# Weight conversion without a maximum and a mask, with a new set of planner settings

## The chip, the cores and the metric

The kernel runs on one NeuronCore of one Trainium2 chip. The core has TensorE for matrix products (PE in the rows, and PEld for its loading of weights), VectorE (DVE), ScalarE (ACT), GpSimd (POOL), and SyncE (SP), whose queue issues every DMA here. The metric is the time of one execution on the device in microseconds (us). Three timed runs of the kernel before took 1967.29, 1968.99 and 1971.42 us, the median being 1968.99 us.

## The reference, cut to what matters

Three layers follow each other. x is 2304 tokens by 512.

```python
x = attention(q, k, v)            # local window of 7 keys, plus attention on means of 4 tokens
h = np.maximum(x @ w_in, 0.0)     # first layer, 512 -> 2048
x = h * h @ w_out                 # 2048 -> 512
P = exp(x @ w_gate - max)         # gates of 8 experts, 8 rounds of balancing rows and columns
for e in range(8):                # second layer
    out += P[:, e:e+1] * (np.maximum(x @ w1[e], 0.0) @ w2[e])
```

The inputs `w_in` and `w_out` of the first layer reach the kernel as 64-bit words (in the host's layout they are viewed as int64, since they are float64), so that the kernel turns each pair of 32-bit words into a float32 itself. This is the weight conversion that the change is about.

## The kernel before, in words

Every fp32 product is made of three products of a high and a low part: the high part is ScalarE's rounding copy, the low part is the rest, a subtraction on VectorE or GpSimd. Tokens are worked in five blocks (`BLOCKS`, j = 0 to 4, of 512, 512, 512, 384 and 384 tokens), and the hidden width of the first layer in 16 pieces of 128 (fc = 0 to 15).

For each block there is an attention part. Blocks 0 and 1 take the local attention on TensorE (`local_pe`, lines 672 to 780, which ends with the matmuls of line 776), blocks 2 to 4 on VectorE (`local_v`, lines 802 to 896, which ends with the transposes of line 867). Attention on the means of four tokens (`down_pair`, lines 555 to 616) has per pair of heads the scores (line 564), three exponentials on ScalarE (line 575), two transposes (line 594) with a ScalarE copy each (line 596), and the product with v (line 609), which ScalarE copies to `od` (line 614). Then come the two products of the first layer (`l1_first`, line 1026; `l2_first`, line 1069), which ScalarE and VectorE join (lines 1041 to 1045). The second layer (`l1_second`, line 1462, and `l2_second`, line 1748) starts when block 4 is done; it needs weights that `units_weights` loads, adds up (line 1284) and splits (line 476), 32 units in all, and for each unit 3 passes of 42 matmuls, with VectorE and ScalarE taking each pass out of PSUM (lines 1529 to 1559).

The conversion of one piece fc (`convert`) loads the 64-bit words of both matrices into one of two buffers `o` (line 936), takes the absolute value of the upper words (ScalarE, line 944), and puts the float32 together on VectorE in four steps (lines 946, 948, 950, 952). Then ScalarE makes the high part `f` (line 957) and VectorE or GpSimd the low part `s` (line 960), which is also stored to DRAM (line 965) and loaded again for the later blocks (line 982).

The order of the instructions on every engine is made when the program is built. `Order` keeps a list of processes, gives each operation the earliest start that a table of costs allows, and writes the instructions down in that order. An engine carries out its list in order, so an instruction that waits holds all that stand behind it on its engine; this includes SP's list of DMAs. The settings of this planner that the diff touches are `AHEAD` (how many pieces ahead the stored low parts are loaded again), `X1FIRST` (how many of four inputs of a block must be there before its first product starts), `NEARLY` (pieces from this number on are converted only after block 0's attention in the plan), `LATE` (by how many ns GpSimd may end later than VectorE and still be given an operation; used in `convert` and `units_weights`) and `SLACK_PE` (ns that TensorE's work of blocks 1 to 4's attention and of the balancing of gates is put later in the plan). Costs that differ also move what is written down.

Of the kernel before, what the change touches and what calls it, by code (L numbers as in the profile page):

```python
# [11 lines left out]
F32 = mybir.dt.float32  # L12
# [4 lines left out]
AF = mybir.ActivationFunctionType  # L17
ALU = mybir.AluOpType
# [23 lines left out]
SCALE = 1.0 / 8.0  # L42
NEG = -1e9

LEAST = float(np.array([896 << 20], np.int32).view(np.float32)[0])

# [26 lines left out]

NVA, NVD, NQD, NDE, NPT = 1, 2, 2, 2, 2

AHEAD, WARM, X1FIRST = 3, 4, 3

NEARLY = 3  # L80

PUT_OFF, PACE = (1, 2, 4), 1


LATE, SLACK, SLACK_PE = 500.0, 100.0, 0.0
LATE_A = 0.0

BOOT_NS, BOOT_DMA = 40000.0, 1.7
# [278 lines left out]
def _dma(nbytes):  # L367
    return ("op", "DMA", nbytes / 360.0)
# [10 lines left out]
def _w2p(n, late=0.0):  # L379
    return ("op", ("V2", "PL"), (148.0 + n * 1.05, 170.0 + n * 2.26), late)  # L380
# [7 lines left out]
def tile_kernel(ctx: ExitStack, tc, qh, kp, vp, qn, kn, vn, vd, bias, mask, w_in, w_out, wg, w12, out):  # L388
    nc = tc.nc
    V, A, PE, PL = nc.vector, nc.scalar, nc.tensor, nc.gpsimd  # L390
# [53 lines left out]
    def get(sl, dt=F32, shape=None, least=1):  # L444
        return ("get", sl, dt, shape, least)
# [478 lines left out]
    def early_half(fc):  # L924
        return int(fc < NF // 2)

    def at_item(j, fc):
        return lambda: (progress["j"], progress["fc"]) >= divmod(j * NF + fc, NF)

    def convert(fc):  # L930

        yield ("need", at_item(0, fc - 5) if fc >= 5 else lambda: len(shared) >= min(NHP, fc + 1))
        raw = yield get(s_boot, I64, [128, 2, 512])
        for i, w in enumerate((w_in, w_out)):
            yield _dma(128 * 4096)
            dma(out=raw[:, i], in_=w[fc])
        if fc >= NEARLY:
            yield ("wait", ev_x1[0][NHP - 1])
        words = raw.bitcast(I32).rearrange("p i (f two) -> p i f two", two=2)
        low, high = words[:, :, :, 0], words[:, :, :, 1]  # L940
        x = yield get(s_x1, F32, None, lambda: 1 + NHP - xs_taken[0])
        xi = x.bitcast(I32)
        yield ("op", "A", 1146)
        A.activation(out=x, in_=raw.bitcast(F32).rearrange("p i (f two) -> p i f two", two=2)[:, :, :, 1], func=AF.Abs)
        yield ("op", "V2", 680)
        V.tensor_scalar(out=x, in0=x, scalar1=LEAST, scalar2=None, op0=ALU.max)
        yield ("op", "V2", 680)
        V.tensor_scalar(out=xi, in0=xi, scalar1=3, scalar2=0x3FFFFFFF, op0=ALU.logical_shift_left, op1=ALU.bitwise_and)
        yield ("op", "V2", 1220)
        V.scalar_tensor_tensor(out=xi, in0=high, scalar=-0x40000000, in1=xi, op0=ALU.bitwise_and, op1=ALU.bitwise_or)  # L950
        yield ("op", "V2", 1220)
        V.scalar_tensor_tensor(out=xi, in0=low, scalar=29, in1=xi, op0=ALU.logical_shift_right, op1=ALU.bitwise_or)
        s_boot.put(raw)
        order.fire(ev_f[fc])
        hi = yield get(s_wf[early_half(fc)], F32R)
        yield ("op", "A", 1146)
        A.activation(out=hi, in_=x, func=AF.Copy)
        lo_ = yield get(gen, F32R)
        eng = ENG[(yield _w2p(1024, LATE))]
        eng.tensor_tensor(out=lo_, in0=x, in1=hi.bitcast(F32), op=ALU.subtract)  # L960
        s_x1.put(x)
        his[fc], los[0, fc] = hi, lo_
        order.fire(ev_w[0, fc])
        yield _dma(128 * 4096)
        dma(out=scr_w[fc], in_=lo_.bitcast(F32))
        order.fire(ev_scr[fc])
        drop_w(0, fc)
# [21 lines left out]
    def drop_w(j, fc):  # L989
        uses[j, fc] -= 1  # L990
        if uses[j, fc] == 0:
            gen.put(los.pop((j, fc)))
# [886 lines left out]
    for fc in range(NF):  # L1879
        order.add(convert(fc), 5.0 + 0.1 * fc)  # L1880
# [63 lines left out]
```

## Time and profile before

| what | value |
|---|---|
| timed runs | 1967.29, 1968.99, 1971.42 us, median 1968.99 us |
| the profiled execution's own time | 1970.68 us |
| its span, from the first to the last instruction | 1968.6 us |
| mean granted TensorE clock | 0.990 of full speed |
| TensorE busy | 1938.3 us (98%) |
| VectorE busy | 1413.1 us (72%) |
| ScalarE busy | 825.0 us (42%) |
| GpSimd busy | 169.8 us (9%) |
| DMA moved | 476.56 MB, mean 242 GB/s |

The profiled execution's own time is 2.1 us over its span and 1.7 us over the median of the timed runs. Busy shares are means over stages with different limits. TensorE's 98% holds filler matmuls too (line 1827, until the first layer starts) and stretches in which the clock was at half speed. A difference of 0.2%, some 3.9 us, is about what a measurement of this kernel tells from none.

### The profile page before, as it was taken

Reading aid. Unit: us, or ns where it says so; the run is one execution under the profiler, and the core shown is the slowest. Engines: PE = TensorE matmul, PEld = TensorE weight load, DVE = VectorE, ACT = ScalarE, POOL = GpSimd, SP = SyncE. Lnnn points to the kernel's source line nnn. Section 1 sums busy time; section 2 is a strip of 40 time slices with the busy share of each in tenths; the row PEclk is TensorE's granted clock in tenths of the full one; section 3 lists DMA queues with packets and bytes.
Section 4 is the critical chain, followed back from the end, with each engine's and each line's share of the span. In section 5 each row is a group of like instructions: output and inputs, shape, how many; then the busy total and the mean of one; then the engine's idle time right before and its main releaser. Section 6 shows DMA issues by size and latency. Waiting matters only on the chain.

```text
span 1968.6 us, 30220 instructions
## 1 busy us (share of the span) xinstructions
PE 1938.3 (98%) x11213; PEld 1841.5 (94%) x11213; DVE 1413.1 (72%) x2002; ACT 825.0 (42%) x1489; POOL 169.8 (9%) x193
## 2 busy tenths in 40 slices
PE   9899989999989999999999999999999999999999
PEld 5677777899989999999999999999999999999998
DVE  6986888883385777777777777777667877666642
ACT  5775443344443222222222222456544454544441
POOL 2101020000001111111111111000001300000000
PEclk9899998999989999999999999999999999999999
DMA  7777665555425665766676666999989999978771
GB/s 205 263 251 243 206 214 172 171 188 199 161 106 202 233 228 209 254 213 229 216 246 224 217 231 230 329 340 336 313 291 339 362 366 336 329 252 276 236 221 49
DMA packets 255148, 476.56 MB, mean 242 GB/s; under 512 B 22248, under 2 KB 163608, under 8 KB 255000
## 3 DMA queue, kind: packets, MB, share of 16 engines
q1 hardware_dynamic: 255000, 474.63, 71.1%
q8 instruction: 88, 1.44, 0.3%
q14 instruction: 60, 0.49, 0.1%
HBM read 306.44 MB, written 168.11 MB: 241 GB/s over the span
## 4 chain that ended last, share of the span: by engine, by line
PE 92%; DMA 4%; DVE 2%; issue 1%; ACT 1%; SPq 0%; POOL 0%; ACTq 0%; DVEq 0%; POOLq 0%
PE b L1462 35%; PE b L1748 34%; PE b L1026 9%; PE b L1069 8%; PE b L1827 1%; DMA r<-scr_h 1%; DMA lk<-in_kp_dram 1%; DMA scr_r<-t 1%; PE b L564 1%; PE b L609 1%; DMA s<-scr_w 0%; PE b L704 0%; PE b L776 0%; DMA o<-in_w_out_dram 0%; PE b L752 0%
## 5 line engine op out<-in xcount | busy, mean ns | idle before, releaser
L1462 PE MATMUL b<-x,w 128*128 128x384 f32 x2112 | 397.2, 338 | 2.4 <-DVE x L476 1.8
L1462 PEld LDWEIGHTS b<-x,w 128*128 128x128 f32 x2112 | 370.2, 189 | 3.6 <-DVE x L476 2.6
L1069 PE MATMUL b<-g,f 128*128 128x512 f32 (+1 forms) x640 | 200.1, 373 | 0.6 <-ACT t L1095 0.6
L1026 PE MATMUL b<-x,f 128*128 128x512 f32 (+1 forms) x640 | 192.1, 381 | 1.5 <-DVE g L1045 1.5
L1462 PE MATMUL b<-xa,w 128*128 128x384 f32 x960 | 188.0, 335 | 0.0
L1529 ACT ACTIVATE b<-b 128x384 f32<-128x384 f32 x96 | 45.6, 475 | 319.8 <-PE b L1462 319.7
L1462 PEld LDWEIGHTS b<-xa,w 128*128 128x128 f32 x960 | 168.4, 188 | 0.3
L1535 ACT ACTIVATE q<-b 128x384 f32<-128x384 f32 x192 | 94.1, 490 | 164.4 <-PE b L1462 162.8
L1748 PE MATMUL b<-q,w 128*128 128x384 f32 x748 | 161.5, 336 | 0.0
L1559 DVE TENSOR_TENSOR q<-b,q 128x384 f32<-128x384 f32 x96 | 53.5, 558 | 117.9 <-PE b L1462 117.9
L1026 PEld LDWEIGHTS b<-x,f 128*128 128x128 f32 x640 | 117.9, 192 | 18.7 <-DVE g L1045 2.8
L1069 PEld LDWEIGHTS b<-g,f 128*128 128x128 f32 x640 | 118.7, 188 | 17.6 <-ACT t L1095 1.2
L1748 PEld LDWEIGHTS b<-q,w 128*128 128x128 f32 x748 | 132.3, 188 | 0.0
L1748 PE MATMUL b<-xa,w 128*128 128x384 f32 x600 | 127.0, 335 | 0.0
L1284 POOL TENSOR_TENSOR w<-w 128x256 f32<-128x256 f32 x60 | 49.9, 831 | 815.5 <-PE b L1462 608.3
L1041 ACT ACTIVATE b<-b 128x512 f32<-128x512 f32 (+1 forms) x160 | 86.8, 542 | 75.8 <-PE b L1026 71.0
L1462 PE MATMUL b<-xc,w 128*128 128x384 f32 x576 | 115.8, 335 | 0.0
L1548 DVE SCALAR_TENSOR_TENSOR q<-b,gp 128x384 f32<-128x384 f32 x178 | 98.7, 555 | 11.5 <-PE b L1462 8.1
L1748 PEld LDWEIGHTS b<-xa,w 128*128 128x128 f32 x600 | 106.0, 188 | 0.0
L1462 PEld LDWEIGHTS b<-xc,w 128*128 128x128 f32 x576 | 101.4, 188 | 0.0
L476 DVE TENSOR_TENSOR q<-r,q 128x768 fp32r<-128x768 f32 x75 | 71.9, 960 | 35.6 <-ACT q L474 35.3
L474 ACT ACTIVATE q<-r 128x768 fp32r<-128x768 f32 x75 | 63.4, 846 | 76.5 <-PE b L1748 35.9
(292 smaller groups left out, 3867.9 us busy)
## 6 DMA issues: line engine op xcount, KB each, us to landing
r<-scr_h SPq DMA_DIRECT2D x240, 384.0 KB
scr_h<-q SPq DMA_DIRECT2D x89, 576.0 KB
gp<-scr_h SPq DMA_DIRECT2D x96, 384.0 KB
scr_h<-q SPq DMA_DIRECT2D x178, 192.0 KB
scr_h<-q SPq DMA_DIRECT2D x89, 384.0 KB
s<-scr_w SPq DMA_DIRECT2D x43, 512.0 KB
w<-in_w_dram SPq DMA_DIRECT2D x64, 256.0 KB
v<-in_w_dram SPq DMA_DIRECT2D x27, 512.0 KB
```

The lines of the kernel that those rows point to most:

```text
L474: A.activation(out=hi, in_=x, func=AF.Copy)
L476: eng.tensor_tensor(out=lo_, in0=x, in1=hi.bitcast(F32), op=ALU.subtract)
L1026: PE.matmul(ps[:, 0:n], lhsT=w[a][:, c], rhs=x[:, b, 0:n], start=(cc == 0 and i == 0), stop=(cc == 3 and i == 2))
L1041: A.activation(out=s, in_=s, func=func)
L1069: PE.matmul(acc[dc][:, 0:n], lhsT=w[a][:, c], rhs=g[:, b, 0:n], start=(fc == 0 and i == 0), stop=(fc == NF - 1 and i == 2))
L1284: eng.tensor_tensor(out=out, in0=in0, in1=in1, op=op)
L1462: PE.matmul(bank[:, 0:TN], lhsT=w[a][:, iw % 4, cc * 128:cc * 128 + 128], rhs=x[:, b, cc], start=(first and cc == 0 and i == 0), stop=(cc ...
L1529: A.activation(out=ps[1][:, 0:TN], in_=ps[0][:, 0:TN], func=AF.Copy)
L1535: A.activation(out=c[:, place], in_=ps[bank][:, 0:TN], func=AF.Copy)
L1548: V.scalar_tensor_tensor(out=c[:, i], in0=ps[bank][:, 0:TN], scalar=0.0, in1=p[:, 0], op0=ALU.max, op1=ALU.mult)
L1559: V.tensor_tensor(out=c[:, 2], in0=ps[0][:, 0:TN], in1=c[:, 2], op=ALU.add)
L1748: PE.matmul(ps[pb][d][:, 0:TN], lhsT=w[a][:, q, d * 128:d * 128 + 128], rhs=h[:, b, q % 2], start=(first and q == 0 and m == 0), stop=(las ...
```

## The change

ScalarE now multiplies the absolute value of the upper words by 2^-112 (`DOWN`), which moves the exponent from the one bias to the other. The maximum of line 946 goes, the mask `0x3FFFFFFF` in the shift goes, and the sign is now taken with the mask -0x80000000 alone. Per piece, VectorE has three steps in place of four, so 16 instructions on 128x1024 elements fewer. One line less in the file moves every later line number by one: line 1026 becomes 1025, 957 becomes 956, and so on.

Five planner settings change as well.

```diff
-LEAST = float(np.array([896 << 20], np.int32).view(np.float32)[0])
+DOWN = 2.0 ** -112
...
-AHEAD, WARM, X1FIRST = 3, 4, 3
-
-NEARLY = 3
+AHEAD, WARM, X1FIRST = 4, 4, 2
+
+NEARLY = 4
...
-LATE, SLACK, SLACK_PE = 500.0, 100.0, 0.0
+LATE, SLACK, SLACK_PE = 1000.0, 100.0, 600.0
...
-        A.activation(out=x, in_=raw.bitcast(F32).rearrange("p i (f two) -> p i f two", two=2)[:, :, :, 1], func=AF.Abs)
+        A.activation(out=x, in_=raw.bitcast(F32).rearrange("p i (f two) -> p i f two", two=2)[:, :, :, 1], func=AF.Abs,
+                     scale=DOWN)
         yield ("op", "V2", 680)
-        V.tensor_scalar(out=x, in0=x, scalar1=LEAST, scalar2=None, op0=ALU.max)
-        yield ("op", "V2", 680)
-        V.tensor_scalar(out=xi, in0=xi, scalar1=3, scalar2=0x3FFFFFFF, op0=ALU.logical_shift_left, op1=ALU.bitwise_and)
+        V.tensor_scalar(out=xi, in0=xi, scalar1=3, scalar2=None, op0=ALU.logical_shift_left)
         yield ("op", "V2", 1220)
-        V.scalar_tensor_tensor(out=xi, in0=high, scalar=-0x40000000, in1=xi, op0=ALU.bitwise_and, op1=ALU.bitwise_or)
+        V.scalar_tensor_tensor(out=xi, in0=high, scalar=-0x80000000, in1=xi, op0=ALU.bitwise_and, op1=ALU.bitwise_or)
```

All engines' lists differ from the first conversions on. Three places matter for what follows.

**TensorE, at the start of the first layer.** In the names, `b6` is PSUM bank 6, which serves the attention on means at this point; `de0_114` are the weights of a pair of heads of that attention that ScalarE has already made. Before, the scores of the next pair (line 564) were written to bank 6 right behind the first nine products of line 1026 and four filler matmuls:

```order
L564 MATMUL b6_161_906<-dp1_135_790,qd1_81 96x144 x3
L704 MATMUL b7_154_891<-pk0_145_841,pq0_144_840 64x70 x8
L706 LDWEIGHTS ident_b_91
L706 MATMUL b7_154_891<-mask_sb_93,ident_b_91 128x280
L1026 MATMUL b5_143_829<-x6_146_845,f1_0_133_779 128x512 x2
```

The transposes of the pair `de0_114` into the same bank came 33 matmuls of the first layer later, one right after the other:

```order
L1026 MATMUL b5_176_988<-x6_146_845,s2_171_961 128x512
L594 MATMUL b6_184_1026<-ident_84,de0_114_649 72x96 x3
L594 MATMUL b6_187_1040<-ident_84,de0_114_649 72x96 x3
L609 MATMUL b6_191_1052<-pt0_170_956,dv1_99_596 64x144 x4
L564 MATMUL b6_195_1068<-dp0_178_1002,qd0_80 96x144 x3
L1026 MATMUL b4_198_1079<-x0_54_385,f1_3_188_1047 128x512 x2
```

Now the transposes stand at the place of those scores, ahead of them, with six or more products between the steps:

```order
L594 MATMUL b6_158_904<-ident_84,de0_114_649 72x96 x3
L1025 MATMUL b5_140_816<-x6_146_849,f1_0_133_772 128x512 x2
L1025 MATMUL b5_140_816<-x6_146_849,s0_136_793 128x512
L1025 MATMUL b4_162_941<-x0_54_385,f1_1_148_854 128x512 x2
L1025 MATMUL b4_162_941<-x0_54_385,s1_155_886 128x512
L1025 MATMUL b4_162_941<-x2_102_605,f1_1_148_854 128x512 x2
L1025 MATMUL b4_162_941<-x2_102_605,s1_155_886 128x512
L594 MATMUL b6_163_944<-ident_84,de0_114_649 72x96 x3
```

The bank is thus read by the older pair first, and the next pair's scores follow later.

**SP, the loads of piece 3.** In the names, `o` is a buffer of 64-bit words, and `scr_w_111<-s_155` (before: `s_155_897`, now `s_155_886`) is the store of piece 1's low part. Before, the second half of piece 3's load (`o_150`, from `w_out`) stood behind that store and three loads for the attention:

```order
L936 DMA o_150_880<-in_w_in_dram 128x512
L497 DMA dr_156_901<-in_qn_dram 128x576
L497 DMA dr_162_916<-in_kn_dram 128x576
L508 DMA vd_163_922<-in_vd_dram 72x1024
L965 DMA scr_w_111<-s_155_897 128x1024
L936 DMA o_150_880<-in_w_out_dram 128x512
L936 DMA o_168_947<-in_w_in_dram 128x512
```

Now both halves (`o_149`) go out ahead of the store, and the attention's loads and the second half of piece 4 (`o_160`) behind it:

```order
L936 DMA o_149_855<-in_w_in_dram 128x512
L936 DMA o_149_855<-in_w_out_dram 128x512
L766 DMA pv_150_872<-in_vn_dram 70x128
L766 DMA pv_150_872<-in_vn_dram 70x7x128
L964 DMA scr_w_111<-s_155_886 128x1024
L936 DMA o_160_932<-in_w_in_dram 128x512
L497 DMA dr_164_949<-in_qn_dram 128x576
```

Piece 3's load moved past the store of piece 1.

**GpSimd, in the first half of the second layer.** `w` are weights of a unit. Before, GpSimd had the four sums of a unit, and VectorE the two splits:

```order
L1284 TENSOR_TENSOR w_1071_6720<-w_1064_6620 128x256
L1284 TENSOR_TENSOR w_1064_6620<-w_1064_6620 128x256
L1284 TENSOR_TENSOR w_1071_6720<-w_1071_6720,w_1064_6620 128x256
L1284 TENSOR_TENSOR w_1071_6720<-w_1064_6620,w_1071_6720 128x256
L1284 TENSOR_TENSOR w_1092_6922<-w_1085_6822 128x256
```

Now the two splits of a unit follow on GpSimd as well:

```order
L1283 TENSOR_TENSOR w_1070_6696<-w_1063_6596 128x256
L1283 TENSOR_TENSOR w_1063_6596<-w_1063_6596 128x256
L1283 TENSOR_TENSOR w_1070_6696<-w_1070_6696,w_1063_6596 128x256
L1283 TENSOR_TENSOR w_1070_6696<-w_1063_6596,w_1070_6696 128x256
L476 TENSOR_TENSOR w_1076_6730<-w_1063_6596,w_1075_6729 128x1024
L476 TENSOR_TENSOR w_1079_6760<-w_1070_6696,w_1078_6759 128x768
```

Over the whole list GpSimd has 59 splits whose result is a tile `w`, where before it had 3, and VectorE has that many fewer.

## Rows read from the trace of the kernel before

**Rows 1.** Windows: stretch, busy us of each engine, TensorE's clock, DMA share, GB/s.
```profile
50.00:75.00 25.00, 19.93 (x142) 13.64 (x142) 22.55 (x33) 16.23 (x38) 4.53 (x6) 0.90 0.79 264
75.00:100.00 25.00, 25.00 (x120) 19.84 (x119) 23.64 (x37) 20.50 (x62) 4.46 (x1) 0.89 0.72 256
250.00:300.00 50.00, 44.49 (x220) 35.88 (x219) 41.90 (x66) 24.51 (x72) 11.97 (x12) 0.89 0.63 206
700.00:1000.00 300.00, 300.00 (x1730) 300.00 (x1729) 228.91 (x358) 81.28 (x150) 43.45 (x56) 1.00 0.67 230
1300.00:1500.00 200.00, 200.00 (x1150) 200.00 (x1149) 137.19 (x171) 100.38 (x119) 0.00 (x0) 1.00 0.95 324
```

**Rows 2.** Chain that ended last, in order of time: start us, us, what.
```profile
71.29 1.70 DVE x L952
73.01 1.06 ACT f L957
...
76.06 4.83 PE b L1026 x12
...
106.33 2.73 PE b L1026 x12
...
597.58 641.10 PE b L1462 x3693
```

**Rows 3.** Waits of TensorE from 60 to 80 us: total us, times, longest.
```profile
PE b L594 <- ACT de L575: 1.4, 1, 1.4
...
PE b L609 <- ACT pt L596: 0.5, 1, 0.5
```

**Rows 4.** Timeline of ScalarE from 63 to 90 us: start, us, what, idle before.
```profile
65.28 1.15 ACT L944 ACTIVATE x<-o 128x1024 f32<-128x1024 f32 x1 [1.25 <-DMA o<-in_w_out_dram]
...
67.78 1.13 ACT L944 ACTIVATE x<-o 128x1024 f32<-128x1024 f32 x1 [0.91 <-DMA o<-in_w_out_dram]
...
68.81 0.37 ACT L575 ACTIVATE de<-b,ti 96x144 f32<-96x144 f32 x1
```

**Rows 5.** Timeline of SP's queue from 51 to 66 us.
```profile
53.74 0.44 SPq L691 DMA_DIRECT2D pk<-in_kn_dram  x1
...
57.04 0.33 SPq L965 DMA_DIRECT2D scr_w<-s  x1
57.42 0.42 SPq L936 DMA_DIRECT2D o<-in_w_out_dram  x1
```

**Rows 6.** Groups by line and shape from 39 to 160 us: count, busy us, mean ns.
```profile
L944 ACT ACTIVATE x<-o 128x1024 f32<-128x1024 f32 x16 | 18.4, 1150 | 9.1 <-DMA o<-in_w_out_dram 8.7 <-DVE s L960 0.4
...
L946 DVE TENSOR_SCALAR x<-x 128x1024 f32<-128x1024 f32 x16 | 11.0, 688 | 4.1 <-ACT x L944 4.0
L948 DVE TENSOR_SCALAR x<-x 128x1024 int32<-128x1024 int32 x16 | 10.9, 683 | 0.1
```

**Rows 7.** Groups of VectorE by line and shape from 600 to 1240 us.
```profile
L476 DVE TENSOR_TENSOR w<-w,w 128x1024 fp32r<-128x1024 f32 x30 | 36.4, 1215 | 2.0 <-ACT w L474 2.0
L476 DVE TENSOR_TENSOR w<-w,w 128x768 fp32r<-128x768 f32 x28 | 26.6, 948 | 0.0
```

**Rows 8.** Groups of GpSimd by line and shape, whole span.
```profile
L476 POOL TENSOR_TENSOR v<-v,w 128x1024 fp32r<-128x1024 f32 x1 | 2.4, 2407 | 95.2 <-ACT w L474 95.2
L476 POOL TENSOR_TENSOR w<-w,w 128x768 fp32r<-128x768 f32 x1 | 1.8, 1847 | 6.1 <-ACT w L474 6.1
```

**Rows 9.** Timeline from 1518 to 1530 us, GpSimd.
```profile
1521.66 3.12 POOL L476 TENSOR_TENSOR v<-w,v 128x1024 fp32r<-128x1024 f32 x1
```

**Rows 10.** Timeline from 1518 to 1530 us, VectorE.
```profile
1520.93 1.58 DVE L476 TENSOR_TENSOR xa<-gp,xa 128x768 fp32r<-128x768 f32 x1
1522.43 3.16 DVE L476 TENSOR_TENSOR q<-gp,q 128x768 fp32r<-128x768 f32 x1
```

**Rows 11.** Line 1559 alone: what VectorE idled for before it, us, times.
```profile
  PE b L1462: 117.9, 93
```

**Rows 12.** Waits of TensorE over the whole span.
```profile
PE b L1193 <- DVE cs L1190: 4.1, 2, 3.3
...
PE b L1129 <- ACT t L1124: 2.7, 1, 2.7
```

## The prediction

> **What bounds the kernel now.** I read the windows first, to see where TensorE lacks time. From 700 to 1000 us and from 1300 to 1500 us it is busy without a gap at full clock [rows 1], and the chain that ended last agrees: line 1462 holds 641.1 us in one piece, 3693 matmuls of 0.174 us, and no other engine stands in it [rows 2]. Those stages can only lose. From 50 to 100 us it is different: TensorE is busy for 19.9 of the first 25 us, its granted clock is 0.90 and then 0.89, while VectorE is busy for 22.6 and 23.6 of 25 us [rows 1]. A mean of 0.9 between the levels 1.2 and 2.4 GHz means some 5 us at the low one in each window.
>
> Next the waits from 60 to 80 us. There are five, from 1.4 to 0.5 us, and together 5.1 us [rows 3]. The timeline of ScalarE says why the longest came: two absolute values (line 944, pieces 3 and 4) stand in its list ahead of the exponentials of a pair of heads (line 575), and both wait for their words by DMA until 65.28 and 67.78 us. The last exponential only starts at 68.81 us [rows 4]. TensorE's transposes (line 594) need PSUM bank 6, which those exponentials read. SP's queue says why the words were late: the second half of piece 3 was issued at 57.42 us, right after the store of piece 1's low part, and that store could not go before VectorE had made the part [rows 5]. From there it took 7.9 us until line 944 ran. The chain closes the circle: at 71.29 us it runs through VectorE's last conversion step and ScalarE's high part of piece 3 [rows 2]. So conversion, its loads and the order of bank 6 set the end in this stretch. The clock fell in it, after these waits, and the next twelve products took 4.83 us, where twelve took 2.73 us later [rows 2].
>
> **The change, part by part.** *The steps of VectorE.* Line 946 goes: 16 x 0.688 = 11.0 us less [rows 6], spread over the first 150 us, where VectorE is over 90% busy. The shift of line 948 loses its second operation. With two it takes 0.683 us, and line 946 with one takes 0.688 us [rows 6], so I give that nothing. The bounds are nothing and the whole step, 10.9 us over 16 pieces, and the nearest row speaks for nothing. ScalarE's absolute value with a scale has no row of this width. Without it, it takes 1.150 us [rows 6], and with ScalarE idle for 8.8 of 25 us [rows 1] even half a microsecond more on each would be covered. I take no change. If that cover were gone, 16 x 0.5 = 8 us would be the price.
>
> *Bank 6 and the loads of piece 3.* The older pair's transposes now come first and have products of the first layer between them, so TensorE no longer waits for exponentials behind line 944. Piece 3's two loads now go out right behind the load of `pk` that was issued at 53.74 us [rows 5], and no longer behind the store of piece 1. That issue took 0.44 us, and the first half needs as long as the 0.42 us of the second [rows 5]; so the second half goes out at 53.74 + 0.44 + 0.42 = 54.6 us, 2.8 us before 57.4. Behind that store, which now waits for GpSimd's subtraction, stand the attention's loads and piece 4's first half; piece 4 has the time of piece 3's products to come.
>
> What comes back: the five waits, 5.1 us, and of the half clock the 4.83 - 2.73 = 2.1 us on twelve products, 7.2 us in all. What I take off: line 609 needs ScalarE's second copy (line 596), which now stands behind line 944 of piece 3. Between nothing and the 2.2 us for which the two absolute values waited [rows 4], I take 1.1 us, halfway, since the load is sooner by 2.8 us but is also wanted sooner. What I add: one line 946, 0.7 us, ahead of the last attention steps that let the first product start. Sum for this stretch: 7.2 - 1.1 + 0.7 = 6.8 us.
>
> *The other settings.* The balancing of gates costs waits of 4.1 us [rows 12]. `SLACK_PE` puts 90 products instead of 84 ahead of TensorE's third sum there, but VectorE's list now has 14 long steps instead of 13 up to it; 6 x 0.174 = 1.0 us against 0.95 us is even. The wait of line 1129 on ScalarE, 2.7 us [rows 12], stays in the order as it was. `AHEAD` loads the stored low parts one piece sooner. For all these I allow 1 us, between nothing and the 4.1 us. The gates end later in the list, so 8 units in place of 7 are finished later from DRAM; their VectorE work and loads fall where TensorE has no gap and DMA is at 0.95 [rows 1]. I price it at nothing, covered by VectorE's 63 idle us of 200 there; if DMA could not carry it, it would cost TensorE a load's wait each time.
>
> *GpSimd's splits.* Per unit, VectorE gives up 1.215 + 0.948 = 2.16 us [rows 7] and GpSimd takes 2.41 + 1.85 = 4.25 us [rows 8]. The trace shows what such a split does to VectorE: one ran on GpSimd from 1521.66 us for 3.12 us [rows 9], and VectorE's subtraction that began at 1522.43 us took 3.16 us [rows 10] instead of 0.95 us. So VectorE may stand still for as long as GpSimd works. This is at most 4.25 - 2.16 = 2.1 us per unit more than before. VectorE idles for 71 of 300 us there [rows 1], that is 5.2 us in the 126 matmuls of a unit, and just before line 1559 it idles 117.9 / 93 = 1.27 us on average [rows 11]. I price this at nothing, hidden by that idle time, with the other side as a rival.
>
> The Trainium skill, "SBUF — State Buffer", section "Who interferes with whom", states that a VectorE instruction with two inputs in SBUF and a GpSimd instruction that reads SBUF exclude each other, and that the one issued first holds the port to its end; the two rows above agree. By that rule alone, with no idle time to hide in, 30 units would pay 2.1 us each, some 63 us, where the rows with their idle time give nothing.
>
> Together 6.8 + 1 = 8 us (7.8). The profiled execution took 1970.68 us, 2.1 us more than its span and 1.7 us more than the median of the runs, 1968.99 us. Taken off that median, 8 us give 1961 us.
>
> **Rivals.** *The lead is eaten (1966.5 us).* Counted in the order, block 1's last attention product (line 776) now has 363 products of the first layer ahead of it, where it had 339: 24 x 0.2275 us = 5.5 us later. VectorE's local attention of block 2 starts only once block 1's inputs are done, and TensorE needs its result at the turn to block 2. Of 8 us then 2.5 remain. For it speaks VectorE's 41.9 of 50 us from 250 to 300 us [rows 1]; against it, that this still leaves 8 us of slack, and that 11.0 us of its work are gone by then.
>
> *More falls away (1950 us).* The turn to block 2 (2.7 us of waiting, clock at 0.89 from 250 to 300 us, so some 11 us at half speed, worth up to 5.5 us [rows 1, 12]) and the balancing (4.1 us) also run through: 2.7 + 5.5 + 4.1 = 12 us more, of which I take 11. Against it: both places have the same steps in nearly the same order.
>
> *Slower (1973 us or more).* GpSimd's two splits of a unit fall into one pass, ahead of line 1559. VectorE is then 2.1 us late against 1.27 us of idle time, TensorE waits for 0.8 us, and 30 units cost 25 us: 1961 + 25 = 1986 us, or 1973 us if half the units are hit. It decides from the point at which what GpSimd holds in a pass is over 1.27 us more than what VectorE gave up. For it speaks rows 10; against it, that half of VectorE's steps there read PSUM and need not wait, and that the splits of a unit are wanted 126 matmuls, 22 us, later.
>
> *The conversion isn't what held it (no change, 1968 us).* If attention's chain on ScalarE sets the pace of the first 80 us, 11.0 us of VectorE buy nothing. The waits for `L575` and `L596` in rows 3 could be read so.
>
> **How the numbers follow.** My forecast, 4 to 12 us faster, has 0.5; more falling away 0.12; the eaten lead and the conversion that did not matter 0.18 together; slower 0.2, most of it through GpSimd's splits, the rest through new waits in a list that has changed everywhere. A change under 0.2%, 3.9 us, can hardly be told from none here. So faster 0.62, same 0.18, slower 0.20. The range runs from 1950 us, where more falls away, to 1973 us, where half the units lose 0.8 us; my forecast's own range is 1957 to 1965 us.
>
> **What would show it.** Right: no line 946; line 1025's first products of piece 3 some 7 us sooner than 76.06 us; no half clock between 70 and 80 us; line 1461 in one piece as long as 641 us, and VectorE's line 1558 with idle time before it. Wrong: a wait at lines 594 or 609 that is as long as before with ScalarE's line 944 in front of it; a lead at 80 us that is gone at 300 us; TensorE waiting for lines 1547 to 1558 from 600 to 1240 us while GpSimd is in line 476.

## The result, and the profile after

The changed kernel is slower. Its median is 1984.87 us (six runs, 1981.42 to 1993.26) against 1969.41 us for the kernel before on the same chip. The ratio on record, 1.0067 with a 95% interval of 1.0047 to 1.0087, is a little less than the two medians alone would give (1.0078), and clear of 1. The prediction was 1961 us, so sign and size were both wrong. The profiled execution has a span of 1985.0 us and a time of 1986.78 us. Against the span before of 1968.6 us that is 16.4 us more.

The windows of after, at the stretches of [rows 1] and at two more, 165 to 215 us and 1500 to 1560 us:

```profile
50.00:75.00 25.00, 22.68 (x152) 16.40 (x152) 20.14 (x29) 16.73 (x43) 6.25 (x5) 0.86 0.89 303
75.00:100.00 25.00, 25.00 (x133) 20.46 (x132) 22.70 (x33) 20.62 (x54) 4.49 (x4) 1.00 0.71 251
165.00:215.00 50.00, 43.46 (x242) 32.73 (x241) 32.68 (x45) 23.86 (x64) 12.55 (x16) 1.00 0.86 265
700.00:1000.00 300.00, 299.90 (x1728) 299.58 (x1727) 225.47 (x328) 80.75 (x150) 105.10 (x82) 1.00 0.65 226
1300.00:1500.00 200.00, 200.00 (x1151) 200.00 (x1150) 136.88 (x172) 98.85 (x117) 0.00 (x0) 1.00 0.94 317
1500.00:1560.00 60.00, 53.72 (x290) 52.31 (x288) 43.60 (x60) 26.20 (x32) 7.21 (x3) 0.94 0.98 346
```

The same two extra stretches in the kernel before:

```profile
1500.00:1560.00 60.00, 58.38 (x343) 57.91 (x342) 49.87 (x56) 31.04 (x41) 24.79 (x9) 1.00 0.98 358
165.00:215.00 50.00, 48.28 (x253) 37.12 (x248) 36.74 (x51) 26.68 (x77) 8.60 (x12) 1.00 0.87 274
```

The start is better, as forecast: TensorE is busy for 22.7 of 25 us instead of 19.9, and from 75 to 100 us its clock is at full. The dense stretches are unchanged. But TensorE is busy 4.8 us less between 165 and 215 us, and 4.7 us less between 1500 and 1560 us, where its clock also falls to a mean of 0.94.

To place the loss I take the start of the k-th product in both traces and subtract the start before. "First layer" counts the matmuls of lines 1025 and 1068, "second half" those of line 1747. A minus means ahead of the kernel before. All kernels of the study stand here once; times are us:

```
                           first layer, product             second half, product
                           60    150    339    550    850   1520   1600   1700
(start before, us)       81.9  108.7  163.8  226.9  320.0 1516.4 1530.4 1551.4
after                    -3.9   -7.7   -5.0    3.0    4.2    5.6   14.8   15.7
after_again              -3.5   -7.2   -6.3    3.0    4.3    5.4   14.8   14.8
seven                    -5.5   -7.6   -5.3    0.6    2.2   11.7   11.7   18.1
before_eight              0.4    0.5    2.1    7.9    7.5    6.7   12.1   13.4
before_slack600           0.6   -0.6   -0.8    6.1   12.5   14.0   24.7   24.2
settings_alone            2.5    0.9   -2.1    1.7   16.6   13.7   19.9   19.9
x1first_three            -3.5   -7.2   -6.3    1.1    0.9    3.3    3.3    6.5
slack_zero               -1.6    0.2   -1.0    1.0    0.9    1.6    1.6    5.8
slack_zero_x1first_three -2.5   -3.3   -4.5   -1.6    2.5    3.3    3.3    3.7
slack_zero_counted_four  -1.2   -2.6   -3.5   -1.0   -1.5   -0.4   -0.4    2.9
slack_zero_late500        5.8    6.8    4.2    5.8    9.9   12.5   12.5   17.5
conversion_alone          5.3    6.9    4.4    8.2    6.0   10.1   10.1    9.8
four_steps_new_order      7.1    8.5    5.9    9.7    8.7   16.0   16.0   16.0
same_order                1.2    1.2    1.4    5.8    3.1    5.2    5.2   11.7
before_again              1.3    1.3    1.4    1.6   -0.3   -0.6   -0.6   -2.4
before_wide               0.8    0.8    2.3    4.4    1.6    0.8    0.8   -1.1
```

After is 7.7 us ahead at product 150. It loses 11.9 us from there to product 850, and 10.2 us more between products 1520 and 1700 of the second half. So of the 16.4 us some 4.2 are there by product 850, 1.4 come from there to product 1520, 10.2 at the second place and the small rest behind it.

The second place is plain in the waits. TensorE from 1500 to 1590 us, after (us in total, times, longest):

```profile
PE b L1747 <- DVE xa L1782: 3.0, 1, 3.0
PE b L1747 <- ACT xa L474: 2.6, 1, 2.6
PE b L1806 <- DVE xc L1785: 1.2, 1, 1.2
PE b L1747 <- DVE xa L476: 0.6, 1, 0.6
```

Behind `ACT xa L474` is a load. The timelines of SP's queue, of VectorE and of ScalarE, after:

```profile
1506.48 2.78 SPq L1599 DMA_DIRECT2D gp<-scr_c  x2
1509.36 0.38 SPq L1604 DMA_DIRECT2D gp<-scr_p  x1
...
1516.85 3.26 SPq L1622 DMA_DIRECT2D scr_h<-gp  x2
...
1522.36 0.45 SPq L1625 DMA_DIRECT2D scr_h<-gp  x1
1522.91 1.53 SPq L1711 DMA_DIRECT2D r<-scr_h  x3
```

```profile
1516.26 1.96 DVE L1612 SCALAR_TENSOR_TENSOR gp<-gp,gp 128x384 f32<-128x384 f32 x4 [3.46 <-DMA gp<-scr_p]
```

```profile
1526.83 0.84 ACT L474 ACTIVATE xa<-r 128x768 fp32r<-128x768 f32 x1 [13.12 <-DMA r<-scr_h]
```

`scr_c` and `scr_p` are the loads of a late unit, the stores to `scr_h` its results, and `r<-scr_h` (line 1711) the hidden rows that the second layer waits for. The stores could not go before VectorE had made what they store, and VectorE had itself idled for 3.46 us until the unit's load of `scr_p` was there. The hidden loads stood behind the stores until 1522.91 us. ScalarE was idle for 13.12 us for the first of them. The kernel before had no late unit left by then. Its queue in the same stretch:

```profile
1497.18 0.46 SPq L1626 DMA_DIRECT2D scr_h<-gp  x1
1497.81 2.33 SPq L1712 DMA_DIRECT2D r<-scr_h  x3
```

The late unit in the first listing is the eighth of eight: the load `gp<-scr_p` stands eight times in SP's list after, and seven times before.

### The profile page after: what moved, and what is told of

It reads as the page before. It is cut to its first block, busy times and chain, and to the rows that moved or that the text cites. A ratio compares the mean times of both kernels' runs of the same rounds, so it can differ in the third digit from the quotient of the medians.

```text
span 1985.0 us, 30125 instructions
## 1 busy us (share of the span) xinstructions
PE 1943.7 (98%) x11207; PEld 1843.5 (93%) x11213; DVE 1399.5 (71%) x1932; ACT 828.2 (42%) x1490; POOL 298.1 (15%) x250
## 4 chain that ended last, share of the span: by engine, by line
PE 81%; DMA 10%; DVE 4%; issue 2%; ACT 1%; SPq 1%; POOL 0%; ACTq 0%; DVEq 0%; POOLq 0%
PE b L1461 33%; PE b L1747 26%; PE b L1068 9%; PE b L1025 9%; DMA r<-scr_h 3%; DMA w<-in_w_dram 1%; PE b L1826 1%; DMA lk<-in_kp_dram 1%; DMA s<-scr_w 1%; DMA o<-in_w_out_dram 1%; DMA gp<-scr_p 1%; DMA scr_r<-t 0%; PE b L704 0%; PE b L564 0%; DMA scr_h<-gp 0%
## 5 line engine op out<-in xcount | busy, mean ns | idle before, releaser
L1461 PEld LDWEIGHTS b<-xa,w 128*128 128x128 f32 x960 | 168.4, 188 | 0.7 <-ACT q L1534 0.6
L476 POOL TENSOR_TENSOR w<-w,w 128x768 fp32r<-128x768 f32 (+1 forms) x57 | 126.2, 2214 | 173.6 <-ACT w L474 173.6
L1494 DVE SCALAR_TENSOR_TENSOR q<-q,gp 128x768 f32<-128x768 f32 x88 | 123.0, 1398 | 3.0
L1747 PEld LDWEIGHTS b<-q,w 128*128 128x128 f32 x688 | 123.0, 188 | 0.0
L1558 DVE TENSOR_TENSOR q<-b,q 128x384 f32<-128x384 f32 x96 | 53.5, 557 | 89.1 <-PE b L1461 89.1
L476 DVE TENSOR_TENSOR q<-r,q 128x768 fp32r<-128x768 f32 x83 | 81.6, 984 | 38.4 <-ACT q L474 38.1
L1747 PE MATMUL b<-q,v 128*128 128x384 f32 x392 | 101.4, 339 | 0.0
```

The costliest lines, as they stand in the source:

```text
L1461: PE.matmul(bank[:, 0:TN], lhsT=w[a][:, iw % 4, cc * 128:cc * 128 + 128], rhs=x[:, b, cc], start=(first and cc == 0 and i == 0), stop=(cc ...
L1494: V.scalar_tensor_tensor(out=x, in0=x, scalar=0.0, in1=p.unsqueeze(1).to_broadcast([128, 2, TN]), op0=ALU.max, op1=ALU.mult)
L1558: V.tensor_tensor(out=c[:, 2], in0=ps[0][:, 0:TN], in1=c[:, 2], op=ALU.add)
L1747: PE.matmul(ps[pb][d][:, 0:TN], lhsT=w[a][:, q, d * 128:d * 128 + 128], rhs=h[:, b, q % 2], start=(first and q == 0 and m == 0), stop=(las ...
```

## The experiments

**Theory 1:** the eighth late unit, which `SLACK_PE` = 600 brings, costs some 10 us near 1530 us. **Theory 2:** a later place of block 1's attention eats the start's lead. **Theory 3:** the conversion is harmless, and the order that the planner writes for a cheaper conversion is what costs. The rivals stand with each run. Where an expectation speaks of six settings, read five.

**seven.** The eighth unit is made an ordinary one; TensorE's order of products stays up to 1546 us, and all first-layer programs stay.

```diff
-        late = ev_rows.at is None
+        late = ev_rows.at is None and units["late"] < 7
         if late:
+            units["late"] += 1
```

> The changed kernel, with the eighth late unit made an ordinary one (it waits for the routing rows, so seven units are put off as before the change). Theory 1: the eighth put-off unit's two loads and four stores stand in the DMA queue ahead of the loads of the second layer's hidden rows, and cost TensorE about 10 us between 1524 and 1545 us; then this kernel takes 1975 us, and its lag behind the kernel before, 5.6 us at product 1520 of the second half, is still 5 to 7 us at product 1600. Rival: that stretch is late for another reason of the new settings (LATE or the GpSimd halves); then 1983 to 1986 us.

Measured 1987.03 us, ratio 1.0080 (1.0065 to 1.0096): no gain. The place answers as theory 1 says: nothing is lost between products 1520 and 1600, where after loses 9.2 us. But the unit, made ordinary, has to wait for the routing rows, and TensorE waits near 610 us:

```profile
PE b L1461 <- DVE q L1561: 5.6, 1, 5.6
```

With that, its lag grew from 2.2 us to 11.7 us before the place, and 6.4 us came between products 1600 and 1700. So the edit put a new cost in place of the old one, and as a test of the time it says nothing.

**before_eight.** The reverse, in the kernel before.

```diff
-        late = ev_rows.at is None
+        late = ev_rows.at is None or units["late"] < 8
         if late:
+            units["late"] += 1
```

> The kernel before, with one unit more put off (eight instead of seven), and nothing else. Theory 1: the eighth unit by itself costs about 10 us at the same place, 1979 us. Rival, the stretch is late because of the other settings: 1969 us as before.

Measured 1981.63 us, ratio 1.0054 (1.0040 to 1.0068), 10.8 us more. The place loses 6.7 us, and SP's queue shows the picture of after:

```profile
1514.37 3.26 SPq L1626 DMA_DIRECT2D scr_h<-gp  x2
...
1519.14 0.45 SPq L1629 DMA_DIRECT2D scr_h<-gp  x1
1519.70 2.19 SPq L1715 DMA_DIRECT2D r<-scr_h  x4
```

The profile is also 7.5 us late by product 850 of the first layer, where its instructions stand in the order of before (up to some 604 us the lists are the same on every engine). That part isn't the eighth unit's; see before_wide.

**conversion_alone.** The changed kernel with all settings as before.

```diff
-AHEAD, WARM, X1FIRST = 4, 4, 2
+AHEAD, WARM, X1FIRST = 3, 4, 3
-NEARLY = 4
+NEARLY = 3
-LATE, SLACK, SLACK_PE = 1000.0, 100.0, 600.0
+LATE, SLACK, SLACK_PE = 500.0, 100.0, 0.0
```

> The new conversion with all six settings as before the change (seven units put off). The planner counts one VectorE step less per piece, so its order differs a little at the start. Theory 2, the three-step conversion gives TensorE 6 to 8 us at the start of the first layer, and what loses it again by product 500 is the later place of block 1's attention that the settings bring: 1962 us. Rival, the lead is lost to VectorE's and the loads' own pace in blocks 1 and 2 whatever the settings: 1967 to 1970 us.

Measured 1983.68 us, ratio 1.0067 (1.0052 to 1.0081). The first half of theory 2 fell with this, that the conversion brings the lead: the start is 6.9 us late at product 150, with seven late units and nothing lost near 1530 us. Whether a later attention eats a lead can't be seen here, where there is none to lose. The loss comes between products 48 and 60, from a lead of 1.1 to a lag of 5.3 us. The timelines of ScalarE and of TensorE there:

```profile
82.57 1.14 ACT L944 ACTIVATE x<-o 128x1024 f32<-128x1024 f32 x1 [0.49 <-DMA o<-in_w_out_dram]
83.60 0.39 ACT L596 ACTIVATE pt<-b 72x288 f32<-72x288 f32 x1
```

```profile
84.04 0.44 PE L594 MATMUL b<-ident,de 96*72 96x96 f32 x3 [3.27 <-ACT pt L596]
```

TensorE's transposes wait for ScalarE's copy of line 596, and ahead of that copy stands the absolute value of the next piece, which waited 0.49 us for its words and took 1.14 us. From 84 to 95 us the clock is at 0.69 after it:

```profile
84.00:95.00 11.00, 10.42 (x45) 8.11 (x46) 9.32 (x14) 9.17 (x27) 0.00 (x0) 0.69 0.63 225
```

**settings_alone.** The kernel before with the new settings.

```diff
-AHEAD, WARM, X1FIRST = 3, 4, 3
+AHEAD, WARM, X1FIRST = 4, 4, 2
-NEARLY = 3
+NEARLY = 4
-LATE, SLACK, SLACK_PE = 500.0, 100.0, 0.0
+LATE, SLACK, SLACK_PE = 1000.0, 100.0, 600.0
```

> The four-step conversion with the new settings (eight units put off). Theory 1 with theory 2: 1969 us, plus 10 us for the eighth unit, plus up to 7 us for the later attention, 1979 to 1990 us. Rival, the loss needs the new conversion: 1969 to 1974 us.

Measured 1992.13 us, ratio 1.0115 (1.0098 to 1.0132), at the upper end of what theories 1 and 2 said. Eight units, 6.2 us lost near 1530 us, and 14.9 us in the first layer between products 550 and 850. Of the rival nothing is left: the settings lose without the new conversion, and more.

**same_order.** The three-step conversion, with the planner still counting four steps. TensorE's, ScalarE's, GpSimd's and SP's programs are then those of the kernel before, and VectorE's lacks 16 instructions.

```diff
         yield ("op", "V2", 680)
+        yield ("op", "V2", 680)
         V.tensor_scalar(out=xi, in0=xi, scalar1=3, scalar2=None, op0=ALU.logical_shift_left)
```

> The kernel before with the new three-step conversion, while the planner still counts four steps: every engine's program is then that of the kernel before, word for word, but for the maximum that is gone from VectorE 16 times. Theory 3 (the conversion itself is harmless, and what costs is the order that the planner writes when it counts three steps): 1963 to 1969 us, since VectorE is ahead by 16 times 0.95 us at most and TensorE waits at the first layer's start for it by 1 to 3 us. Rival (with one step less VectorE only comes sooner to a wait for ScalarE's absolute value, 5.9 us of such waits in the run with the conversion alone, and the start is late by it): 1975 to 1984 us.

Measured 1973.15 us over 12 runs, ratio 1.0010 (0.9995 to 1.0025): no difference. The profiled execution, 1982.65 us, was the slowest of the 12. VectorE's and ScalarE's steps of the conversion from 39 to 160 us (busy us, mean ns, idle before and for what):

```profile
L944 ACT ACTIVATE x<-o 128x1024 f32<-128x1024 f32 x16 | 18.5, 1155 | 7.1 <-DMA o<-in_w_out_dram 6.7 <-DVE s L960 0.4
L948 DVE TENSOR_SCALAR x<-x 128x1024 int32<-128x1024 int32 x16 | 10.9, 683 | 0.6 <-ACT x L944 0.6
```

The maximum's 11.0 us are gone, the wait for line 944 didn't grow against [rows 6], the scale costs ScalarE nothing (1.155 us against 1.150), and the simpler shift is no shorter (0.683 us both). TensorE got nothing from it: product 150 is 1.2 us late, and in two other profiles of that order it is 0.8 and 1.3 us late (before_wide, before_again). So in that order the step that was removed did not hold TensorE.

**four_steps_new_order.** The old conversion, counted as three steps.

```diff
         V.tensor_scalar(out=x, in0=x, scalar1=LEAST, scalar2=None, op0=ALU.max)
-        yield ("op", "V2", 680)
         V.tensor_scalar(out=xi, in0=xi, scalar1=3, scalar2=0x3FFFFFFF, op0=ALU.logical_shift_left, op1=ALU.bitwise_and)
```

> The four-step conversion, with the order that the planner writes when it counts three steps: the programs of the run with the conversion alone, with a maximum more on VectorE 16 times. Theory 3: as slow as the conversion alone or a little slower, 1983 to 1990 us. Rival (the three-step conversion itself is what costs): 1969 to 1974 us.

Measured 1988.96 us, ratio 1.0091 (1.0069 to 1.0112). The maximum is back, and the order alone costs 17 us. Theory 3 holds: conversion_alone is slow by its order. In this order the three steps may be worth 1988.96 - 1983.68 = 5.3 us, but the intervals of the two ratios overlap, so that isn't shown.

**slack_zero.** The changed kernel with one setting back.

```diff
-LATE, SLACK, SLACK_PE = 1000.0, 100.0, 600.0
+LATE, SLACK, SLACK_PE = 1000.0, 100.0, 0.0
```

> The changed kernel with SLACK_PE back at 0, the other settings new: seven units are put off, and block 1's first attention group stands three products earlier. Theory 1 (the eighth put-off unit costs 5 to 10 us near 1530 us): the late stretch at products 1520 to 1700 of the second half is gone or under 2 us, 1975 to 1980 us. Rival (any order other than that of the kernel before loses there or elsewhere by as much): 1983 to 1990 us.

Measured 1974.62 us over 12 runs, ratio 1.0010 (0.9994 to 1.0027). The 10 us come back with this one number, though it moves more than the late unit: the lists part from those of after at 50 us, the lead of the start is gone too, and at product 1520 this kernel is 1.6 us late where after is 5.6. Nothing is lost between products 1520 and 1600; the 4.1 us between 1600 and 1700 are over the 2 us that I wrote. So some 6 of the 10 us come back at the place of the late unit, and 4 ahead of it.

**after_again.** A second profile of the changed kernel.

> The changed kernel again, for a second profile. What is of its order repeats: ahead of the kernel before by 5 to 9 us at product 150 of the first layer, 3 to 5 us behind at product 850, 9 to 11 us more lost between products 1520 and 1700 of the second half. What is chance moves by several us between the two profiles.

The two agree within 1.3 us at every product of the table: the lead, its loss and the 9.4 us near 1530 us belong to the program.

**x1first_three.** The changed kernel with `X1FIRST` at 3. Its programs are those of after until 272 us, late in block 1, `SLACK_PE` stays, and the planner puts off seven units by itself.

```diff
-AHEAD, WARM, X1FIRST = 4, 4, 2
+AHEAD, WARM, X1FIRST = 4, 4, 3
```

> The changed kernel with X1FIRST back at 3 and SLACK_PE still 600: the engines' programs are those of the changed kernel through most of block 1, and this time the planner itself puts off seven units. Theory 1 (what SLACK_PE costs is the eighth put-off unit): 1973 to 1979 us, with 0 to 4 us lost between products 1520 and 1700 of the second half. Rival (SLACK_PE costs by the later attention in the first layer, and the eighth unit only takes part of it): 1981 to 1987 us, with a lag of 4 us or more by product 850 of the first layer.

Measured 1973.11 us, ratio 1.0014 (1.0002 to 1.0026), as theory 1 says. From product 1520 to product 1700 it loses 3.2 us, 6.9 us less than after, and none of it before product 1600. Its queue issues the hidden rows at 1501.92 us, 21 us sooner than after:

```profile
1501.28 0.54 SPq L1625 DMA_DIRECT2D scr_h<-gp  x1
1501.92 1.74 SPq L1711 DMA_DIRECT2D r<-scr_h  x3
```

The start's lead of 7.2 us is lost here as well, 0.9 us behind at product 850. It doesn't make the kernel slower than before, it only isn't kept.

**before_slack600.** The kernel before with one new setting.

```diff
-LATE, SLACK, SLACK_PE = 500.0, 100.0, 0.0
+LATE, SLACK, SLACK_PE = 500.0, 100.0, 600.0
```

> The kernel before with SLACK_PE at 600 and nothing else: four-step conversion, eight units put off. Theory 1: 1979 to 1984 us, 5 to 10 us of it between products 1520 and 1700 of the second half, as in the run with eight units in the kernel before. Rival (SLACK_PE only costs together with the new conversion): 1969 to 1973 us.

Measured 1990.41 us, ratio 1.0099 (1.0082 to 1.0117), more than I wrote. The place near 1530 us takes 10.2 us, at the upper end of what I expected. Another 12.5 us are there by product 850, most of it waits of line 1026 for VectorE's line 1045 (7.9 us in two). That part I had not foreseen.

**slack_zero_late500.** slack_zero with one more setting back.

```diff
-LATE, SLACK, SLACK_PE = 1000.0, 100.0, 0.0
+LATE, SLACK, SLACK_PE = 500.0, 100.0, 0.0
```

> The changed kernel with SLACK_PE 0 and LATE 500, that is without most of the halves on GpSimd. Theory (GpSimd's halves cost nothing that TensorE waits for): 1972 to 1978 us, as with SLACK_PE 0 alone. Rival of the prediction (the longer steps on both engines cost 4 us or more): 1964 to 1970 us.

Measured 1981.70 us, ratio 1.0052 (1.0032 to 1.0073): slower than slack_zero, against both sides of my expectation. It falls into the wait of conversion_alone (line 594 for line 596, 2.8 us), from 0.2 us ahead at product 48 to 5.8 us late at product 60. So `LATE` = 1000 doesn't cost on balance here; with it the planner writes another order.

**slack_zero_x1first_three.** slack_zero with the edit of x1first_three.

```diff
-AHEAD, WARM, X1FIRST = 4, 4, 2
+AHEAD, WARM, X1FIRST = 4, 4, 3
```

> The changed kernel with SLACK_PE 0 and X1FIRST 3: only the conversion, LATE, AHEAD and NEARLY are new. Theory (X1FIRST moves little once seven units are put off): 1972 to 1978 us. Rival (the earlier second-layer products of X1FIRST 2 are what loses the start's lead): 1964 to 1970 us, faster than the kernel before.

Measured 1977.80 us, ratio 1.0030 (1.0016 to 1.0045). The lead of 3.3 us at product 150 goes, so the rival is out.

For three more runs the open question was why before_eight is late in a part that it shares with the kernel before, and what eats the lead.

**before_again.** The kernel before, a second profile. The 47 us are those from just behind product 339 to product 500 (165.2 to 212.5 us).

> The kernel before again, for a second profile. If its quick passage between first-layer products 339 and 600 (47 us less than any other kernel by 4 us) belongs to its program, the two profiles agree within 1.5 us there; if it was chance, the second one is 3 to 8 us later at product 600, as the kernels with the same first-layer program were.

At the products of the table the two profiles are within 1.6 us of each other until product 1600, and its second profile took 1968.26 us; the quick passage isn't one lucky execution.

**before_wide.** The same programs, other places in DRAM.

```diff
-            h = dr.tile([128, 4, TN], F32, name=f"scr_c{u}_{pb}")
+            h = dr.tile([128, 8, TN], F32, name=f"scr_c{u}_{pb}")
...
-            dma(out=h, in_=c)
+            dma(out=h[:, 0:4], in_=c)
```

> The kernel before with each put-off unit's DRAM tensor twice as large and only its first half used: every engine's program stays, only where tensors lie in DRAM changes. If the first layer's 5 to 8 us in the runs with eight units and with the same order come from where things lie, this run loses some of it too, 1974 to 1980 us; if they come from those kernels' programs, 1969 to 1973 us and a first layer within 2 us of that of the kernel before.

Measured 1970.53 us, ratio 1.0003 (0.9986 to 1.0020): this placement doesn't matter. Its first layer was 4.4 us late at product 550, over the 2 us that I allowed if the programs were the cause, and 1.6 us at product 850. So this much can change between executions of the same programs.

**slack_zero_counted_four.** slack_zero with the count of same_order.

```diff
         yield ("op", "V2", 680)
+        yield ("op", "V2", 680)
```

> The changed kernel with SLACK_PE 0, while the planner still counts four steps in the conversion. Theory 3 (the cheaper count moves the first layer's order and loses there): 1965 to 1972 us. Rival (each new order is a fresh draw about 1975 us): 1973 to 1982 us.

Measured 1974.59 us, ratio 1.0019 (1.0005 to 1.0033), that of slack_zero. With `LATE` = 1000 the count matters no more, and theory 3's loss is one of certain orders, not of the count.

No kernel of the study beats the kernel before; slack_zero, same_order and before_wide can't be told from it.

## Why the prediction was wrong, step by step

**The start** came out near the forecast: 6.8 us said, 7.7 us found. Some 2.4 us of that are no gain, since at product 150 the new order has put 51 attention matmuls fewer behind it (by their times in the kernel before, an estimate); with equal work the lead is some 5.3 us. TensorE's five waits [rows 3] have become one from 60 to 80 us:

```profile
PE b L1025 <- DVE g L1044: 2.3, 1, 2.3
```

The chain in order of time runs on TensorE without a gap from there, nine products at 67.57 us still at half clock, and from 74.90 us twelve in 2.73 us:

```profile
67.57 4.14 PE b L1025 x9
71.70 1.14 PE b L564 x6
72.84 2.06 PE b L1068 x9
74.90 2.73 PE b L1025 x12
```

The half clock did not go, it moved and grew shorter: 0.57 on average from 65 to 73 us, 6.8 us at the low level where it was 10.2 us before. My sum had all five waits and the half clock gone, so that the size came near is in part luck. The reason that I gave, fewer VectorE steps, is not shown. In the order of before the removed step is worth nothing (same_order), and settings_alone, which has four steps and so another order, is 0.9 us late where after is 7.7 us ahead. No run kept the order of after with four steps, so what of the lead is the order's and what the conversion's stays open. Part of what VectorE saved has turned into a wait for ScalarE, 8.2 us where line 946 waited for 4.1 us [rows 6], and ScalarE waits for DMA. The groups of after, 39 to 160 us:

```profile
L944 ACT ACTIVATE x<-o 128x1024 f32<-128x1024 f32 x16 | 18.3, 1146 | 11.0 <-DMA o<-in_w_out_dram 10.5 <-DVE s L959 0.5
...
L947 DVE TENSOR_SCALAR x<-x 128x1024 int32<-128x1024 int32 x16 | 11.0, 689 | 8.2 <-ACT x L944 8.2
```

**The first step that failed** is to carry the 6.8 us to the end. That was the rival "the lead is eaten", with 5.5 us; it took all of it and 4.2 us more. What I gave for it, VectorE's local attention of block 2 coming later, is where it shows, but ahead of the turn to block 2 at which I placed it: 8.0 us go between products 339 and 550, and 1.2 us from there to product 850, over that turn. TensorE waits from 160 to 320 us, after:

```profile
PE b L1128 <- ACT t L1123: 6.0, 2, 4.6
PE b L1025 <- DVE g L1044: 3.0, 1, 3.0
PE b L1115 <- ACT de L575: 1.6, 1, 1.6
PE b L564 <- POOL dp L534: 1.2, 1, 1.2
```

One of VectorE's own waits there, 165 to 240 us, names the loads of block 2:

```profile
DVE lp L823 <- DMA lk<-in_kp_dram: 5.3, 2, 3.1
```

Line 1044 stands in VectorE's list behind line 823, which waits for `lk`, as its timeline shows for TensorE's wait of 3.0 us:

```profile
210.99 2.03 DVE L823 TENSOR_TENSOR lp<-lq,lk 128x1792 f32<-128x1792 f32 x1 [3.06 <-DMA lk<-in_kp_dram]
...
213.02 0.66 DVE L1044 TENSOR_TENSOR g<-b,g 128x512 fp32r<-128x512 f32 x1
```

SP issued the first load of `lk` at 172.76 us after and at 168.44 us before, although TensorE was 5.0 us ahead at product 339: a lead on TensorE's products didn't bring the loads forward. In SP's list they stand behind a load of `m`, and that one waited in both kernels for block 1's last attention products (line 776). Before, and then after:

```profile
164.09 1.15 PE L776 MATMUL b<-pa,pv 70*64 70x64 f32 x32
165.32 0.35 SPq L982 DMA_DIRECT2D m<-scr_w  x1
```

```profile
167.72 1.15 PE L776 MATMUL b<-pa,pv 70*64 70x64 f32 x32
168.96 0.32 SPq L981 DMA_DIRECT2D m<-scr_w  x1
```

The new order has these products 3.6 us later, as the rival had it with its 24 more products ahead of them. No run moved them alone, and it is not the whole of it: in slack_zero these products start later still, at 170.04 us, the first load of `lk` goes out at 175.96 us, and product 550 is only 1.0 us late. Executions that share the first layer's order suggest what these waits are worth. Waits for `lk` from 165 to 215 us of 4.2 us (before), 3.8 (before_again), 5.4 (before_wide), 7.3 (same_order) and 7.9 us (before_eight) go with 0, 0.1, 2.1, 4.4 and 5.8 us lost between products 339 and 550. Why the last two wait longer is not settled, nor is the part that X1FIRST and SLACK_PE have in after's loss beyond its lead; no run gave block 2's loads another place. The wait of line 1129, which I kept at 2.7 us [rows 12], grew to 6.0 us in two.

**The second step that failed** is the late unit: "I price it at nothing, covered by VectorE's 63 idle us of 200 there". The cover was on VectorE, and the cost fell on SP's queue. With eight units the place loses 10.2, 9.4, 10.2, 6.7 and 6.2 us, with seven between -1.8 and 6.5 us over eleven profiles. The ends touch: some 3 to 6 us can come between products 1600 and 1700 with seven units too, from the sums of line 1785. From product 1520 to product 1600 alone they lie apart: all five profiles with eight units lose 5.4 to 10.7 us, and all eleven with seven lose nothing. In the time, either setting that takes the eighth unit away gives back 10 to 12 us (slack_zero, x1first_three), of which 6 to 7 us are at this place in their profiles. I did write what it would cost if DMA could not carry it, a load's wait each time, but gave that no place, no price and no chance.

**The 1 us for the other settings** did not come either. The balancing's waits of 4.1 us [rows 12] are no longer among TensorE's, but from 480 to 660 us line 1461 waits for the parts of `x`, 5.4 us where before it was 1.8 us:

```profile
PE b L1461 <- ACT x L474: 3.0, 2, 2.0
PE b L1461 <- DVE x L476: 2.4, 2, 1.7
```

**GpSimd's splits**, the rival on which the chance of slower rested, cost next to nothing. There are 57 of the two common shapes in after, a little longer than [rows 8] say:

```profile
L476 POOL TENSOR_TENSOR w<-w,w 128x1024 fp32r<-128x1024 f32 x28 | 71.8, 2563 | 102.8 <-ACT w L474 102.8
L476 POOL TENSOR_TENSOR w<-w,w 128x768 fp32r<-128x768 f32 x29 | 54.4, 1877 | 70.8 <-ACT w L474 70.8
```

TensorE's only wait from 600 to 1240 us is one of 0.3 us. The idle time before VectorE's line 1558, which was to hide them, shrank from 117.9 us [rows 11] to 89.1 us and was not used up:

```profile
  PE b L1461: 89.1, 85
```

VectorE did pay: its gating of line 1494 (1495 before) took 1414 ns instead of 956 ns, which is 85 x 0.458 = 39 us in the stretch from 600 to 1240 us. Before:

```profile
L1495 DVE SCALAR_TENSOR_TENSOR q<-q,gp 128x768 f32<-128x768 f32 x87 | 83.2, 956 | 2.0
```

and after:

```profile
L1494 DVE SCALAR_TENSOR_TENSOR q<-q,gp 128x768 f32<-128x768 f32 x85 | 120.2, 1414 | 2.9
```

It had given up 36.4 + 26.6 = 63 us of splits there [rows 7], so it is the better for it, if by little: from 700 to 1000 us it was busy for 225.5 us instead of 228.9 us. The Trainium skill, "SBUF — State Buffer", section "Who interferes with whom", states that the two engines exclude each other on such instructions. The trace agrees: the 28 of line 1494 that ran at the same time as a split took 2340 ns on average, the other 57 took 959 ns. The 63 us that the rule would have cost TensorE with no idle time to hide in did not come.

## What to carry to other kernels

A unit of work that is moved has to be followed through every queue that it uses, and here what was queued behind its last store mattered more than how idle the engine was that computed it. A lead at the start is not yet time at the end: here the loads of the next stage went out no sooner, so look at what their queue waits for ahead of them before adding the lead to the end. Where a planner writes the order, separate an instruction's cost from the order that its changed cost brings: keep the count and change the code, and the reverse.

## What was not expected of the hardware

After two waits of 2.6 and 3.0 us near 1527 and 1540 us TensorE's clock fell each time; from 1524 to 1534 us the mean is 0.83, from 1538 to 1547 us 0.81, and the 10.2 us lost there are more than the 7.4 us of waits. The scale on ScalarE's absolute value was free (1146 ns and 1155 ns a step against 1150 ns), and so was the second operation of VectorE's shift (689 ns and 683 ns without it, 683 ns with it).
